# Attention, Fourier mix and FFN on one core: the second FFN matmul as seven block products in place of eight, for ten pairs of token chunks

## The chip, the core and the metric

The kernel runs on one core of a Trainium2 chip. The core has five engines, each with an instruction stream of its own: TensorE (PE; its weight loads are listed apart as PEld), VectorE (DVE), ScalarE (ACT), GpSimd (POOL) and SyncE (SP), which only issues transfers. They wait for one another by semaphores. Matmuls read SBUF and write PSUM, whose eight banks hold 512 fp32 values per partition. The metric is the time of one execution on the device in microseconds (us), less is better. The kernel before took 610.42, 608.97 and 610.12 us; the median is 610.12.

## The reference

Eight batches, 12 heads, 448 rows, 64 columns per head; D = 768 = 12 x 64; the FFN's inner width is 3072. All inputs and the output are fp32.

```python
scores = scale * np.matmul(q, k.transpose(0, 1, 3, 2))
attn = np.maximum(scores, 0.0) ** 2 / S
x = np.matmul(attn, v)                  # heads side by side: [8, 448, 768]
mixed = np.real(np.fft.fft(np.fft.fft(x, axis=1), axis=2))
u = x + mixed
un = (u - mean(u)) / np.sqrt(var(u) + 1e-06)
out = u + np.maximum(un @ w_ch1, 0.0) @ w_ch2      # 768 -> 3072 -> 768
```

The two FFN matmuls are done on 8 x 448 = 3584 rows, called tokens below.

## The kernel before

**How the order is made.** The program's order is written by a planner in Python that runs when the kernel is built. Each part of the work is a generator that asks for a step with `need(engine, duration, deps, bufs, ok)` (L104) and emits its instructions when the planner (`Streams.run`, L78) gives it its turn. The planner takes the step that could start first by its estimates; `ok` holds a step back while it is false. What comes out is one fixed order per engine, with semaphore waits between engines. On the chip every engine executes its own order strictly. SP's stores, loads and transposes are one such order, and GpSimd's loads and indirect stores are part of GpSimd's.

**Attention and mix, batch by batch.** Scores (L537, PSUM psS), relu (ACT, L558), square (DVE, L564), values (L522, PSUM psF). The result leaves PSUM as xT (DVE, L445 and L448); SP transposes it to rows, xn (L477); folds and differences (L456 to L468) halve the Fourier transform; the channel transform is L961, its copies pc L977, the row transform L805. A batch's half rows come in two chunks of 128 and 112. For each chunk and for top and bottom half, `mix_rows` makes qs (L811), tm and tp (L816), u = mix + xn (L825, L826, on POOL and DVE), statistics (L837, L838), std (L841), rstd (L844), nmr (L846) and un = u x rstd + nmr (L854, on POOL from batch 2). u and un go to DRAM: top rows from SP (L876), bottom rows in reverse order by indirect stores from POOL (L879). SP loads un back transposed as unT (L902), which is the moving operand of the first FFN matmul.

**The FFN in groups.** `ffn(b)` works on groups of 384 and 512 tokens in turn, eight in all; two groups cover two batches. A group's unT needs the un of its last batch. FFN1 (L1073): 24 inner blocks of 128, each six matmuls of 128 x N into one psF bank, then relu into hT (L1046 on ACT; L1044 on DVE for odd blocks of the first group). FFN2 (L1091): per chunk of 128 tokens and per half of 384 output columns, 24 matmuls accumulate in one psF bank, then DVE adds u, loaded into o by `reload` (SP, L1034), at L1054, and SP stores o (L1061). The last chunk of all is cut into 512 and 256 columns. PSUM: three two-bank tiles psS, two one-bank tiles psF.

**Attention between FFN work.** Attention steps of later batches (six scores, eight values matmuls) stand between FFN matmuls on TensorE. Their `ok` is a comparison of the FFN's progress with `lead`, the attention's progress less `LEAD = 1.9` batches. When the FFN of the group that needs batch b's un begins, TensorE's next FFN1 matmul waits for that unT; nothing of TensorE's order is moved for it.

**Buffers.** In SBUF: sq nine buffers, un four (two chunks by top and bottom), u two for each half, unT two, hT 24 tiles, o two of 768 columns.

Of the kernel before, what the change touches and what calls it, by code (L numbers as in the profile page):

```python
# [62 lines left out]
class Streams:  # L63
    def __init__(self):
        self.engine = dict.fromkeys(LATENCY, 0.0)
        self.streams = []
        self.dma_free = {"sw": 0.0, "hw": 0.0}
# [11 lines left out]
    def run(self):  # L79
        end = {}  # L80
        while self.streams:
# [7 lines left out]
            best = None  # L89
            for s in self.streams:  # L90
# [9 lines left out]
                if best is None or key < best[0]:  # L100
                    best = (key, s)
            if best is None:
                assert not self.streams, "stuck"
                break  # L104
            (_, start, _), s = best
# [32 lines left out]
def kernel(  # L138
# [26 lines left out]
    XH = 256  # L165

# [27 lines left out]
    warm = const.tile([128, 512], BF16, name="warm")  # L194
# [3 lines left out]
    dcol = work.tile([128, 2 * KH], FP32, name="dcol", tag="tm", bufs=1)  # L198
# [43 lines left out]
    def build_dft():  # L242
# [19 lines left out]
        f = work.tile([128, 4 * KH], FP32, name="dfty", tag="u", bufs=2)  # L262
        g = work.tile([128, 4 * KH], FP32, name="dfty", tag="u", bufs=2)
# [6 lines left out]
        for m in range(3):  # L270
            e = yield need("DVE", 1.5, [indices_ready])
            y = work.tile([128, 4 * KH], FP32, name="dfty", tag="u1" if m < 2 else "o", bufs=2)
            turns(y[:, 2 * KH:], y[:, 0:2 * KH], col2, row[:, 4 + m:5 + m], 2 * KH, m % 2)
            yield from sine(chan[m][:, 0, :], y[:, 0:2 * KH], 2 * KH, e, -1, halfpi)
            yield from sine(chan[m][:, 1, :], y[:, 2 * KH:], 2 * KH, e)
# [8 lines left out]
    BQ = [Bufs(QN), Bufs(QN), Bufs(3)]  # L284

    def load_group(i, which=(0, 1, 2)):
# [3 lines left out]
        for x, (nm, src) in enumerate((("q", q), ("k", k), ("v", v))):  # L290
# [5 lines left out]
            else:  # L296
                e = yield need("POOL", 0.85, bufs=[BQ[x]])
                t = work.tile([R, HG, 4 * Dh], BF16, name=f"{nm}n", tag=f"{nm}n",
                              bufs=3 if nm == "v" else QN)
# [19 lines left out]
    first_qk = [work.tile([128, NG, HG, 4 * Dh], BF16, name="qk0", tag="unT", bufs=2) for _ in range(2)]  # L319
# [43 lines left out]
    BSQ = Bufs(NSQ)  # L363
    BX = [Bufs(1) for _ in range(MC)]
# [5 lines left out]
    progress = [0.0]  # L370
# [6 lines left out]
    def turning():  # L377

        for b in range(B):
            for g in range(NG):  # L380
# [5 lines left out]
                for x in range(2):  # L386
# [3 lines left out]
                    BQ[x].free.append(e)  # L390
# [15 lines left out]
    def turn_on_pe(b, g):  # L406
# [23 lines left out]
        if b > 0:  # L430
            BQ[0].free.append(e1)
            BQ[1].free.append(e1)
        elif g == NG - 1:
            BUNT.free += [e1, e1]
# [4 lines left out]
    def fold(b, m, F, av, av_end):  # L439
        e1 = yield need("DVE", 2 * dve(HS) + 2 * dve2(NS), [av_end],  # L440
                        [BX[m]] + ([BA[m]] if m < 3 else []))
        x = xTc[m]

        at = av[:, 0:S].rearrange("q (j p) -> q p j", j=4)
        nc.vector.tensor_scalar(x[:, 0:HS].rearrange("q (p j) -> q p j", j=4), at[:, 0:R // 2],  # L445
                                1.0 / (64.0 * S), None, op0=ALU.mult)
        xb, ab = x[:, XH + 1:XH + NS].rearrange("q (p j) -> q p j", j=4), at[:, R - 1:R // 2 - 1:-1, ::-1]
        nc.vector.tensor_scalar(xb, ab, 1.0 / (64.0 * S), None, op0=ALU.mult)  # L448
        BF.give(av, e1 - 2 * dve2(NS))
        if b > 0:  # L450
            sch.add(turn_x(b, m, e1 - 2 * dve2(NS) + LATENCY["DVE"]), (1, 1))
        else:
            x_ready[b][m].t = e1 + LATENCY["DVE"]
        f = work.tile([128, 2, NS], BF16, name="fold", bufs=1,
                      tag=f"diff{m - 3}" if b == 0 and m >= 3 else f"fold{min(m, 3)}")
        nc.vector.tensor_tensor(f[:, 0, :], x[:, 0:NS], x[:, XH:XH + NS], op=ALU.add)  # L456
        nc.vector.tensor_tensor(f[:, 1, :], x[:, 0:NS], x[:, XH:XH + NS], op=ALU.subtract)
# [4 lines left out]
        elif m >= 3:  # L462
            i = m - 3
            e1 = yield need("DVE", 2 * dve2(2 * NS))
            t = work.tile([128, 2, NS], BF16, name="diff", tag=f"diff{i}", bufs=1)
            nc.vector.tensor_tensor(t, F[i], f, op=ALU.subtract)
            Bs[b].append(t)
            nc.vector.tensor_tensor(F[i], F[i], f, op=ALU.add)  # L468
# [13 lines left out]
    def attention(b):  # L482


        F, sqs, fresh = [], {}, []
        NB = 4 * MC
        p = pa = 0
        while pa < NB:
# [7 lines left out]
            n = max(0, min(n, NSQ - (p - pa - 4 * values)))  # L496
# [15 lines left out]
            e = yield need("PE", dur + SWITCH, deps, bufs, lambda: progress[0] >= lead and (b != 1 or tail[0] == 2 or tail[0] == 0 and p < 0))  # L512
            av_end, scs = None, []

            for part in ("scores", "values") if few else ("values", "scores"):
                if part == "values" and values:
                    av = BF.take()
                    vn, h0 = loads[b * NG + ma // 2][2], 2 * ma % HG
                    for c in range(4):
                        sq = sqs.pop(pa + c)[0]  # L520
# [26 lines left out]
            for i, _, _ in scs:  # L547
                sqs[i] = [None, Cell()]
# [5 lines left out]
    def squares(scs, sqs):  # L554
        for i, sc, t in scs:
            e = yield need("ACT", act(2 * S) - 0.03, [t + LATENCY["PE"]], [BSQ])
            r = sqs[i][0] = work.tile([R, 2, S], BF16, name="sq", tag="sq", bufs=NSQ)
# [9 lines left out]
    def attentions():  # L567
        for b in range(1, B):
            yield from attention(b)


    BU, BTS = [Bufs(2), Bufs(2)], Bufs(1)
    BPC, BUN = Bufs(1), [Bufs(1), Bufs(1)]
    group_ready = [Cell() for _ in range(B)]
# [4 lines left out]
    groups = []  # L579

    def first_tail(pcs):
# [70 lines left out]
        def copy(t, hf, en):  # L652
            ch, i = divmod(t, 2)
            n = SC[ch][1] - SC[ch][0]
            e = yield need(en, (act if en == "ACT" else dve)(D // 2), [done[t][hf]], [BU[i]] if hf == 0 else [])
            if hf == 0:
                uts[t] = work.tile([128, D], FP32, name="u", tag=f"u{i}" if i else "u", bufs=2)
# [127 lines left out]

    half_un, u_done = ([[Cell(), Cell()] for _ in range(2)] for _ in range(2))
# [10 lines left out]
    def mix_rows(b, ch, pcs):  # L797
# [14 lines left out]
        e = yield need("DVE", 2 * dve(KN), [e + LATENCY["ACT"]])  # L812
        ts = []
        for op, nm in ((ALU.subtract, "tm"), (ALU.add, "tp")):
            t = work.tile([128, 2 * KH], FP32, name=nm, tag=nm, bufs=1)
            nc.vector.tensor_tensor(t[:n, 0:KN], pq[:n, 0, 0:KN], qs[:n], op=op)  # L816
            ts.append(t)
# [3 lines left out]
        for i, eng, en, d in ((1, nc.gpsimd, "POOL", 1.8), (0, nc.vector, "DVE", 2 * dve(KN))):  # L821
            e1 = yield need(en, d, [e + LATENCY["DVE"]] + x_ready[b], [BU[i]])
            x = xns[b][:, 2 * i + ch, :]
            u = work.tile([128, D], FP32, name="u", tag=f"u{i}" if i else "u", bufs=2)
            eng.tensor_tensor(u[:n, 0:KN], ts[i][:n, 0:KN], x[:n, 0:KN], op=ALU.add)  # L825
            eng.tensor_tensor(u[:n, KN:D], ts[1 - i][:n, KN - 2:0:-1], x[:n, KN:D], op=ALU.add)  # L826
# [6 lines left out]
        for i, u in enumerate(us):  # L833
            e = yield need("DVE", 2 * dve(D // 2) + 0.2, [ut[i]])
            stats = work.tile([128, 2, 6], FP32, name="stats", tag="stats", bufs=2)
            for hf in range(2):
                nc.vector.bn_stats(stats[:n, hf, :], u[:n, hf * (D // 2):(hf + 1) * (D // 2)])  # L837
# [4 lines left out]
        e = yield need("DVE", 0.3, [e3 + LATENCY["ACT"]], [BUN[ch]])  # L842
# [5 lines left out]
        for i, u in enumerate(us):  # L848
# [3 lines left out]
            un = work.tile([128, D], BF16, name="un", tag=f"un{2 * ch + i}", bufs=1)  # L852
# [31 lines left out]
    def u_store(b, ch, us, ut, freed):  # L884
        yield from store_rows(ch, utop[b], ubot[b], us, 4, ut, u_stored[b])
        yield need("SP", 0.0, freed)
        for i in range(2):
            BU[i].free.append(max(u_stored[b][2 * ch + i].t, freed[i].t))

    def n_store(b, ch, t):  # L890
        yield from store_rows(ch, ntop[b], nbot[b], uns[b][2 * ch:2 * ch + 2], 2,
                              [t, t], n_stored[b])
        if b > 0:
            BUN[ch].free.append(n_stored[b][2 * ch + 1].t)

    def turn_un(b):

        def turn(g, c0, src, r0, w, deps, bufs=()):
            e = yield need("SP", 1.5, deps, bufs)
            if g is None:  # L900
                g = work.tile([128, MC, 512], BF16, name="unT", tag="unT", bufs=2)
# [3 lines left out]
        n = n_stored[b]  # L905
# [5 lines left out]
        elif b % 2 == 0:  # L911
            g, _ = yield from turn(None, 0, ntop[b], 0, HS, [n[0], n[2]], [BUNT])
            _, e = yield from turn(g, HS, nbot[b], 0, 384 - HS, [n[1], n[3]])
            groups.append((b * S, 384, g))
        else:
# [247 lines left out]
```

## Time and profile before

| | us |
|---|---|
| median of 3 runs (608.97 to 610.42) | 610.12 |
| span of the profiled execution | 607.4 |
| TensorE busy | 595.4 |
| VectorE busy | 339.4 |
| ScalarE busy | 293.3 |
| GpSimd busy | 155.2 |
| FFN1 matmuls L1073, busy | 227.2 |
| FFN2 matmuls L1091, busy | 225.0 |
| FFN groups begin at | 53.7, 126.7, 210.7, 272, 350.7, 413.5, 490.7, 541.7 |

The profiled execution's own span, 607.4 us, is from its first to its last instruction; the times of the runs include what lies around it. Busy times of groups of matmuls overlap a little, as matmuls are pipelined, and a few matmul records are missing. So one matmul's cost is read from the distance between the starts of two stretches, not from its duration.

### The profile page before, as it was taken

Reading aid. Unit: us, or ns where it says so; the run is one execution under the profiler, and the core shown is the slowest. Engines: PE = TensorE matmul, PEld = TensorE weight load, DVE = VectorE, ACT = ScalarE, POOL = GpSimd, SP = SyncE. Lnnn points to the kernel's source line nnn. Section 1 sums busy time; section 2 is a strip of 40 time slices with the busy share of each in tenths; the row PEclk is TensorE's granted clock in tenths of the full one; section 3 lists DMA queues with packets and bytes.
Section 4 is the critical chain, followed back from the end, with each engine's and each line's share of the span. In section 5 each row is a group of like instructions: output and inputs, shape, how many; then the busy total and the mean of one; then the engine's idle time right before and its main releaser. Section 6 shows DMA issues by size and latency. Waiting matters only on the chain.

```text
span 607.4 us, 10224 instructions
## 1 busy us (share of the span) xinstructions
PE 595.4 (98%) x4035; PEld 329.5 (54%) x4054; DVE 339.4 (56%) x766; ACT 293.3 (48%) x445; POOL 155.2 (26%) x200
## 2 busy tenths in 40 slices
PE   8999999989999999999999999999999999999997
PEld 7566556534555565555445565555445566654464
DVE  6977785876596568455834369645843447110011
ACT  5967661677544357436653167435761345014300
POOL 8433203311163137111710117210620006100000
PEclk9999999999999999999999999999999999999999
DMA  9999997888659967977593796985451215420022
GB/s 127 207 209 228 216 194 132 186 128 120 111 148 212 157 121 215 141 135 120 172 154 96 127 127 173 160 164 97 145 136 60 87 51 165 121 91 20 1 79 79
DMA packets 125216, 82.22 MB, mean 135 GB/s; under 512 B 76272, under 2 KB 113168, under 8 KB 125168
## 3 DMA queue, kind: packets, MB, share of 16 engines
q0 software_dynamic: 40320, 34.07, 34.4%
q1 hardware_dynamic: 84848, 47.50, 33.6%
q8 instruction: 32, 0.52, 0.4%
q14 instruction: 16, 0.13, 0.1%
HBM read 62.91 MB, written 26.69 MB: 148 GB/s over the span
## 4 chain that ended last, share of the span: by engine, by line
PE 83%; DVE 11%; ACT 4%; issue 1%; DVEq 0%; ACTq 0%
PE psF L1091 33%; PE psF L1073 32%; PE psF L522 6%; PE psS L537 6%; DVE sq L564 2%; PE psS L961 2%; ACT sq L558 2%; DVE stats L837 2%; PE psS L1113 1%; PE psS L805 1%; DVE u L826 1%; DVE u L825 1%; PE psS L605 1%; PE psF L421 1%; DVE tm L816 1%
## 5 line engine op out<-in xcount | busy, mean ns | idle before, releaser
L1073 PE MATMUL psF<-unT,w 128*128 128x384 bf16 (+1 forms) x1134 | 227.2, 352 | 1.4 <-issue 0.2
L558 ACT ACTIVATE sq<-psS 112x896 bf16<-112x896 f32 x192 | 164.8, 916 | 130.5 <-PE psS L537 130.4
L1091 PE MATMUL psF<-w,hT 128*128 128x384 bf16 (+2 forms) x1343 | 225.0, 326 | 0.8 <-DVE xT L448 0.7
L1091 PEld LDWEIGHTS <-hT 128*128 128x128 bf16 x1344 | 129.2, 98 | 93.4 <-issue 8.8
L1073 PEld LDWEIGHTS <-w 128*128 128x128 bf16 x1152 | 109.6, 98 | 109.3 <-issue 12.3
L1046 ACT ACTIVATE hT<-psF 128x512 bf16<-128x512 f32 (+1 forms) x180 | 98.6, 548 | 110.2 <-PE psF L1073 109.6
L564 DVE TENSOR_TENSOR sq<-sq 112x896 bf16<-112x896 bf16 x192 | 117.8, 635 | 44.6 <-ACT sq L558 43.3
L1054 DVE TENSOR_TENSOR o<-psF,o 128x384 f32<-128x384 f32 (+2 forms) x56 | 31.0, 553 | 106.2 <-PE psF L1091 105.9
L300 POOL DMA_DIRECT2D vn<-in_v_dram x24 | 17.3, 719 | 177.4 <-PE psF L522 156.9
L445 DVE TENSOR_SCALAR xT<-psF 128x224 bf16<-128x224 f32 x48 | 18.7, 389 | 71.7 <-PE psF L522 71.7
L537 PE MATMUL psS<-qkT 64*112 64x448 bf16 x384 | 52.3, 366 | 2.0 <-DVE unT L780 0.8
L522 PE MATMUL psF<-sq,vn 112*64 112x448 bf16 x384 | 45.9, 359 | 1.7 <-DVE sq L564 1.2
L825 POOL TENSOR_TENSOR u<-tp,xn 128x385 f32<-128x385 f32 (+1 forms) x14 | 15.5, 1108 | 117.0 <-DVE tp L816 94.7
L537 PEld LDWEIGHTS <-qkT 64*112 64x112 bf16 x384 | 20.8, 125 | 27.6 <-issue 21.6
L522 PEld LDWEIGHTS <-vn 112*64 112x64 bf16 x384 | 17.9, 109 | 24.2 <-issue 16.0
L854 POOL TENSOR_SCALAR un<-u,rstd,nmr 128x768 bf16<-128x768 f32 (+1 forms) x24 | 26.9, 1124 | 6.4 <-DVE nmr L846 6.0
L837 DVE BATCH_NORM_STATS2 stats<-u 128x6 f32<-128x384 f32 (+1 forms) x56 | 28.2, 539 | 0.0
L879 POOL DMA_INDIRECT ubot<-u,back x16 | 17.1, 1072 | 23.7 <-DVE hT L1044 19.3
L300 POOL DMA_DIRECT2D qn<-in_q_dram x21 | 15.3, 726 | 19.7 <-DVE qkr L389 10.8
L1113 PE MATMUL psS<-warm 128*128 128x126 bf16 (+1 forms) x204 | 17.9, 242 | 1.3 <-DVE warm L215 1.3
L448 DVE TENSOR_SCALAR xT<-psF 128x224 bf16<-128x224 f32 x48 | 18.4, 384 | 0.0
L456 DVE TENSOR_TENSOR fold<-xT 128x225 bf16<-128x225 bf16 x48 | 15.9, 331 | 2.1
(117 smaller groups left out, 369.1 us busy)
## 6 DMA issues: line engine op xcount, KB each, us to landing
out_dram<-o SPq DMA_DIRECT2D x27, 384.0 KB, 2.7
vn<-in_v_dram POOLq DMA_DIRECT2D x24, 224.0 KB, 5.0
qn<-in_q_dram POOLq DMA_DIRECT2D x21, 224.0 KB, 6.3
kn<-in_k_dram POOLq DMA_DIRECT2D x21, 224.0 KB, 7.2
w<-in_moe_w_ch_dram POOLq DMA_DIRECT2D x12, 384.0 KB, 14.1
w<-in_moe_w_ch_dram POOLq DMA_DIRECT2D x4, 1152.0 KB, 22.7
utop<-u SPq DMA_DIRECT2D x8, 384.0 KB, 2.6
o<-utop SPq DMA_DIRECT2D x8, 384.0 KB, 4.5
```

Of the source, the lines that this page charges most:

```text
L300: nc.gpsimd.dma_start(out=t, in_=src[b, hs].rearrange("h (p j) d -> p h (j d)", j=4))
L522: nc.tensor.matmul(av[h * Dh:(h + 1) * Dh, 0:S], lhsT=vn[:, c, h0 + h, :], rhs=sq[:, h, :], start=(c == 0), stop=(c == 3))
L537: nc.tensor.matmul(sc[:R, h, 0:S].rearrange("k (c q) -> k c q", c=4), lhsT=kT[ps, m % 2, c, :], rhs=qT[ps, m % 2], start=True, stop=True)
L558: nc.scalar.activation(r, sc[:R, :, 0:S], AF.Relu)
L564: nc.vector.tensor_tensor(r, r, r, op=ALU.mult)
L837: nc.vector.bn_stats(stats[:n, hf, :], u[:n, hf * (D // 2):(hf + 1) * (D // 2)])
L854: nc.gpsimd.tensor_scalar(un[:n], u[:n], rstd[:n, i:i + 1], nmr[:n, i:i + 1], op0=ALU.mult, op1=ALU.add)
L1046: nc.scalar.activation(h[:, 0:N], ph[:, 0:N], AF.Relu)
L1054: nc.vector.tensor_tensor(o[:, hs], pc[:, 0:w], o[:, hs], op=ALU.add)
L1073: nc.tensor.matmul(ph[:, 0:N], lhsT=w1_sb[m][hf][:, jj * 128:(jj + 1) * 128], rhs=unT[:, m, 0:N], start=(m == 0), stop=(m == MC - 1))
L1091: nc.tensor.matmul(pc[:, 0:w], lhsT=hT[j][:, c * 128:(c + 1) * 128], rhs=w2_sb[j // 6][:, j % 6, hs], start=(j == 0), stop=(j == JC - 1))
L1113: nc.tensor.matmul(first_pps[0][:, t, c0:512], lhsT=warm[:, 0:128], rhs=warm[:, c0:512], start=not begun, stop=False)
```

## The change

Split the 16 first inner blocks into eight pairs (even, odd), the 768 output columns into two halves, and take two chunks of 128 tokens, L and R. Then these 16 blocks of FFN2 are a product of a 2 x 2 by a 2 x 2 matrix of blocks, in which each block product is eight matmuls of 128 x 384. The usual way needs eight block products. The new one needs seven (Winograd's form), with sums of the operands:

- of the weights, once (`weight_sums`, 32 adds of 128 x 384 on POOL): T3 = B22 - B12, T2 = T3 + B11, T4 = B21 - T2, and T1 = B12 - B11 in place over the weights themselves;
- of the hidden values, per pair, on DVE: s1 = R_even + R_odd, s2 = s1 - L_even, and R_even replaced by L_even - R_even (`early`); L_odd replaced by L_odd - s2 after product b1 has read it (`late`). Each is made in two pieces, of 768 and of 256 columns;
- of the products, in PSUM and in the output tiles: a bank is added to one output tile, then goes on accumulating the next product, is added to the next tile, and so on. Eight adds per pair in place of four.

The other eight inner blocks (`rest`) are done as before. TensorE's order in a pair is a1 (8 matmuls), b1 (16), a2 (8), b2 (8), a3 (8), b3 (16), a4 (16), b4 (8): 88 matmuls in place of 96. It is done for ten pairs in the groups that are not `PLAIN`; FFN2 goes from 1344 to 1264 matmuls of 384 columns.

With it come:

- nine groups of 384, 512, 256, 512, 512, 512, 256, 512 and 128 tokens. In FFN1 two inner blocks share a bank where N is 256, four where it is 128;
- room for the sums: the weight sums lie in unT0 (so one unT tile is left from the third group on), in two u and u1 buffers, in two sq buffers and in the first q and k buffers. From batch 3 on both chunks of a batch use one pair of un buffers and one pair of u buffers; sq has six buffers in place of nine. tm is no longer a tile of its own, qs is overwritten. s1 and s2 lie in the other un buffers;
- hT as one tile [128, 24, 512]; the output in pieces of 384 columns in six slots, each loaded, added to and stored by itself (`outputs`). SP has 262 instructions in place of 193;
- `load_left`: four loads on POOL bring back the weights that T1 has overwritten, for the last, plain group;
- in the planner: LEAD 2.3, `APART` (the gated attention steps at least 1.3 us of FFN work apart), `fill` (a gated attention step is taken early when TensorE's next step would otherwise start over 0.5 us later), and from batch 3 the steps of fold and mix_rows are planned one instruction at a time (`next_step`).

TensorE's order is the same as before up to the second group's FFN1.

```diff
+    GT = [0, 384, 896, 1152, 1664, 2176, 2688, 2944, 3456, B * S]
+    KP = 8
...
+            if best[1][2][0] == "PE" and spare is not None and best[0][1] - spare[0][1] > 0.5:
+                best = spare
...
+        room = NSQ if b < 3 else NSQ - 3
...
+    def side(b, ch):
+        return ch if b < 3 else 1
...
-        e = yield need("DVE", 0.3, [e3 + LATENCY["ACT"]], [BUN[ch]])
+        e = yield need("DVE", 0.3, [e3 + LATENCY["ACT"]], [BUN[ch if b < 3 else 0]])
...
-            un = work.tile([128, D], BF16, name="un", tag=f"un{2 * ch + i}", bufs=1)
+            un = work.tile([128, D], BF16, name="un", tag=f"un{2 * (ch if b < 3 else 0) + i}", bufs=1)
...
+    PLAIN = (0, 1, NGR - 1)
+    CH = [(0, 6), (6, KP)]
...
+    def weight_sums():
...
+        def each(n, outs, xs, ys, op, deps):
+            T[n] = outs
+            for i in range(KP):
+                e = yield need("POOL", 1.3, deps)
+                nc.gpsimd.tensor_tensor(outs[i], xs[i], ys[i], op=op)
+            sums[n].t = e + LATENCY["POOL"]
...
+        yield from each(3, t3, b22, b12, ALU.subtract, [])
...
+        yield from each(2, t2, t3, b11, ALU.add, [sums[3]])
...
+        yield from each(4, t4, b21, t2, ALU.subtract, [sums[2]])
+        yield from each(1, b12, b12, b11, ALU.subtract, [w2_free, sums[3]])
...
+    def outputs(slot):
+        for g, c, hf, at in uses():
...
+            e = yield need("SP", 0.1, stored + [ffn_begun[g]])
...
+                nc.sync.dma_start(out=o[t - t0:t - t0 + w], in_=src[r:r + w, cs])
...
+            e = yield need("SP", 0.1, [added[g, c, hf]])
+            nc.sync.dma_start(out=rows[t0:t0 + 128, cs], in_=o)
...
+        for j in range(0, JC, JN):
...
+            for i in range(JN):
+                for m in range(MC):
+                    nc.tensor.matmul(ph[:, i * N:(i + 1) * N], lhsT=w1_sb[m][hf][:, (jj + i) * 128:(jj + i + 1) * 128],
+                                     rhs=unT[:, m, 0:N], start=(m == 0), stop=(m == MC - 1))
...
+        def early(self):
...
+                nc.vector.tensor_tensor(s1, h[:, ev, R_], h[:, od, R_], op=ALU.add)
+                nc.vector.tensor_tensor(s2, s1, h[:, ev, L], op=ALU.subtract)
+                nc.vector.tensor_tensor(h[:, ev, R_], h[:, ev, L], h[:, ev, R_], op=ALU.subtract)
...
+        def late(self):
...
+                nc.vector.tensor_tensor(h[:, self.od[k], L], h[:, self.od[k], L], made[1][k], op=ALU.subtract)
...
+        def chain_a(self):
...
+            self.product(pc, self.block(0, self.L), self.weights(0, 0), True)
+            t = yield from self.add(pc, e, c, 0, False, False)
...
+            self.product(pc, self.formed(1), T[2], False)
+            t = yield from self.add(pc, e, c + 1, 0, False, False)
...
+            self.product(pc, self.formed(0), T[1], False)
+            t = yield from self.add(pc, e, c + 1, 1, False, False)
+            e = yield need("PE", d + dr, [t] + self.r4 + self.ht[2 * KP:])
+            self.product(pc, self.block(1, self.L), self.weights(1, 1), False)
+            self.rest(pc, self.L, 1, False)
+            yield from self.add(pc, e, c, 1)
...
+        def chain_b(self):
...
+            self.product(pc, self.block(1, self.L), self.weights(1, 0), True)
+            self.rest(pc, self.L, 0, False)
+            yield from self.add(pc, e, c, 0)
...
+            self.product(pc, self.block(0, self.R), T[3], True)
+            t = yield from self.add(pc, e, c + 1, 1, False, False)
...
+            self.product(pc, self.block(1, self.R), T[4], False)
+            self.rest(pc, self.R, 0, False)
+            yield from self.add(pc, e, c + 1, 0)
...
+            self.rest(pc, self.R, 1, True)
+            yield from self.add(pc, e, c + 1, 1)
...
-    LEAD = 1.9
+    LEAD = 2.3
...
+        sch.fill = lambda: progress[0] > 2.0
```

More of the change, by code (lines that the diff above doesn't have):

```diff
@@ L439, in fold @@
     def fold(b, m, F, av, av_end):
[L440 to L447, printed above, removed]
@@ L811, in mix_rows @@
         nc.scalar.activation(qs[:n], pq[:n, 1, 0:KN], AF.Copy)
[L812 to L817, printed above, removed]
+        e = yield need("DVE", (2 if b < WHOLE else 1) * dve(KN), [e + LATENCY["ACT"]])
+        tp = work.tile([128, 2 * KH], FP32, name="tp", tag="tp", bufs=1)
+        nc.vector.tensor_tensor(tp[:n, 0:KN], pq[:n, 0, 0:KN], qs[:n], op=ALU.add)
+        e = yield from next_step(b, "DVE", dve(KN), e)
+        nc.vector.tensor_tensor(qs[:n], pq[:n, 0, 0:KN], qs[:n], op=ALU.subtract)
+        ts = [qs, tp]
         BS.give(pq, e)
@@ L1068, in ffn, with add @@
-        for j in range(JC):
+            for x in ht[j:j + JN]:
+                x.t = e + LATENCY["ACT"]
+        def add(pc, e, c, hf, last=True, give=True):
+            e = yield need("DVE", dve(DH), [e + LATENCY["PE"], ot[b, c, hf]])
+            o = os[b, c, hf]
+            nc.vector.tensor_tensor(o, pc[:, 0:DH], o, op=ALU.add)
+            if give:
+                BF.give(pc, e)
+            if last:
+                added[b, c, hf].t = e + LATENCY["DVE"]
+            return e + LATENCY["DVE"]
```

394 lines of the change are left out of this document (285 added, 109 removed).

## The prediction

> **What bounds the kernel now.** I read the page's busy shares and slices first.
>
> ```profile
> PE 595.4 (98%) x4035; PEld 329.5 (54%) x4054; DVE 339.4 (56%) x766; ACT 293.3 (48%) x445; POOL 155.2 (26%) x200
> ...
> PE   8999999989999999999999999999999999999997
> ...
> DVE  6977785876596568455834369645843447110011
> ...
> PEclk9999999999999999999999999999999999999999
> ```
>
> TensorE is busy for 595.4 of 607.4 us at a full granted clock. Of the 12 us left, about 8 lie before 158 us, so there is no idle time left to win behind it: time falls if TensorE gets less work, and rises with every new wait of TensorE. The profiled execution spans 607.4 us and the median of the runs is 610.12, so 2.7 us lie around the span; I sum against 607.4 and add 2.7.
>
> Next the timeline, for durations. Columns: start, duration, engine, line, operation.
>
> ```profile
> 48.33 0.71 PE L706 MATMUL psS<-warm 128*128 128x256 bf16 x5
> 48.88 0.34 PE L708 MATMUL psS<-rev,un 128*128 128x63 bf16 x6
> 49.05 1.06 PE L713 MATMUL psS<-warm 128*128 128x128 bf16 x16
> 49.94 0.49 PE L706 MATMUL psS<-warm 128*128 128x256 bf16 x3
> ...
> 502.62 15.86 PE L1073 MATMUL psF<-unT,w 128*128 128x384 bf16 x96
> ...
> 518.31 23.56 PE L1091 MATMUL psF<-w,hT 128*128 128x384 bf16 x144
> ...
> 541.71 31.24 PE L1073 MATMUL psF<-unT,w 128*128 128x512 bf16 x141
> 572.79 31.36 PE L1091 MATMUL psF<-w,hT 128*128 128x384 bf16 x191
> ```
>
> From start to start: FFN2, 144 matmuls of 384 columns, 518.31 to 541.71, 0.1625 us each. FFN1 at 384: 15.69/96 = 0.163; at 512: 31.08/144 = 0.216. The rows of 48 to 50 us give 0.11 (256 columns) and 0.056 (128 columns, each with its own weight load).
>
> Last the way of a batch's second chunk of rows into the next group, for batches 3 and 7.
>
> ```profile
> 236.86 0.16 DVE L846 SCALAR_TENSOR_TENSOR nmr<-mv,rstd 112x2 f32<-112x2 f32 x1
> 237.13 2.51 POOL L854 TENSOR_SCALAR un<-u,rstd,nmr 112x768 bf16<-112x768 f32 x2 [0.38 <-DVE nmr L846]
> 239.91 1.03 POOL L879 DMA_INDIRECT nbot<-un,back  x1 [0.28 <-POOL un L854]
> 244.30 3.26 SPq L902 DMA_TRANSPOSE unT<-nbot  x1
> 247.65 4.05 SPq L477 DMA_TRANSPOSE xn<-xT  x2
> ...
> 514.22 0.16 DVE L846 SCALAR_TENSOR_TENSOR nmr<-mv,rstd 112x2 f32<-112x2 f32 x1
> 515.57 1.93 POOL L854 TENSOR_SCALAR un<-u,rstd,nmr 112x768 bf16<-112x768 f32 x2
> 518.15 0.96 POOL L879 DMA_INDIRECT nbot<-un,back  x1 [0.65 <-POOL un L854]
> 521.28 1.33 SPq L902 DMA_TRANSPOSE unT<-nbot  x1
> ```
>
> ```profile
> DMA to landing us min/median/max: 2.5/4.3/8.9
> ```
>
> That last line is of the unT transposes (L902), the rows below of busy time by stretch (PE, PEld, DVE, ACT, POOL).
>
> ```profile
> 126.70:157.90 31.20, 31.04 (x166) 13.31 (x169) 18.11 (x44) 22.11 (x33) 5.73 (x9) 1.00 0.89 126
> 157.90:210.70 52.80, 52.04 (x343) 28.22 (x343) 36.43 (x82) 24.64 (x34) 17.65 (x18) 1.00 0.82 158
> ...
> 350.70:413.50 62.80, 62.55 (x419) 35.21 (x418) 42.67 (x93) 33.42 (x55) 19.19 (x21) 1.00 0.88 153
> ```
> In batch 7 the second chunk's transpose lands near 525 (521.28 + 3.4) and group 7 begins at 541.71: 16 us of slack. The change shortens the work that covers this way.
>
> **The change, part by part.**
>
> *FFN2's products.* A pair takes 56 + 32 = 88 matmuls in place of 96; ten pairs drop 80. 80 x 0.1625 = **-13.0 us**, all on TensorE.
>
> *FFN1's columns.* Before: 576 x 0.163 + 576 x 0.216 = 218.3. After: 144 x 0.163 + 720 x 0.216 + 288 x 0.11 + 144 x 0.056 = 218.7: **+0.4**. The 128-column group is the uncertain one: were its matmuls paced like the mix's (24 of 193 columns in 2.0 us, 0.083), it would add 3.9 more. I take 0.056, as that burst also loads weights each time, and keep 0 to +4. [...]
>
> *VectorE.* A pair costs 8 adds of 0.553 (L1054's row) in place of 4, and 8 bf16 sums: four of 768 elements, four of 256, by the squares' row (896 in 0.635) 0.54 and 0.2. That is 5.2 us more per pair, 52 in all. It is hidden while VectorE keeps up: from 350.7 to 413.5 it is busy 42.7 of 62.8; with two pairs 53.1 of about 60, 88%. It doesn't bound, but queues get longer. Inside a pair each product of chain a waits for the add behind the one before (handoff 0.25 + add 0.55 + 0.1 = 0.9) while the other chain's product covers 8 x 0.1625 = 1.3. Cover suffices unless the add stands behind a square (0.635) or a mix operation (u 0.55, bn 0.54): then it misses by 0.2 to 0.8. Some five pairs have such work beside them; I take **+1.4** (0 to 4).
>
> *GpSimd.* 32 weight sums (bf16, 128x384) run between about 126 and 220 us. GpSimd's add of 385 fp32 columns takes 0.9 to 1.3, so 29 to 42 us in a stretch where GpSimd is busy 23 of 84: they fit. But two-input adds on both engines stretch each other: VectorE's u at 503.68 takes 0.55, at 504.14, beside GpSimd's u (503.85, 1.15), 1.27. Lower bound 0 (VectorE is busy 54.5 of the 84); upper, 3. I take **+1.0**. [...]
>
> *Group 2 is 256 tokens long, and group 3 needs batch 3's second chunk.* Only one pair of FFN2 lies between. By the instruction order of the changed kernel, VectorE does nmr of that chunk behind the add that follows a4, the seventh of eight product blocks. TensorE has after a4: values 0.95, scores 0.78, b4 1.3, values 0.95, scores 0.78 = 4.8, and then the first matmul of group 3. From a4's end to unT: handoff, add, rstd, nmr 0.25 + 0.55 + 0.16 + 0.16; to un 0.3; un 1.93 to 2.51; nbot's issue 0.3 later, to the transpose's start 3.1 (518.15 to 521.28) to 4.4; landing 2.5 to 6.5 (what the batch-2 transpose took). Sum 9.3 to 15.1, with the median landing of 4.3 about 11.8: TensorE waits 7. A second way gives the same: on SP's queue this transpose is behind an xn transpose that waits for xT copied from the last values, so -0.78 + 0.25 + 0.78 (two xT) + 1.22 + 1.33 + 4.3 = 7.1. Batch 7's landed in 3.4, so I take 3.3, a us less: **+6.0** (4.0 to 10). Nothing fills it: TensorE's order is fixed.
>
> *Group 6 is 256 tokens long, group 7 needs batch 7's second chunk.* On SP the nbot7 transpose stands behind the output store of b4, the pair's last product, which waits for its add; group 7's first matmul comes right after b4. So the wait is 0.25 + 0.55 + store issue 0.35 + 0.2 + landing 2.5 to 4.3 = 3.9 to 5.7. The data is no earlier: both chunks now use one un and one u pair of buffers, so the second waits until the first's stores have landed (ubot 4.4 us, nbot 3.5 after issue). **+4.8.** In the same pair b2 waits for an add behind u and bn: **+0.5**.
>
> *Other homes.* Six sq buffers instead of nine from batch 3, one unT tile: groups 4, 5 and 8 have 4 us and more between data and use by the same counting, since 512 tokens of work lie between; 0. The output's 384-column pieces make SP issue 262 instead of 193; a store is 0.35 and SP is waited for nowhere else that I counted: 0. Four loads on GpSimd's queue (0.72 each) bring back original weights for the last group while GpSimd is idle (its slices read 0 at the end): 0.
>
> *Tail.* The last add is 384 columns (0.55 for 0.42) and the last store 192 KB, between 1.7 (128) and 2.0 (256): **+0.4**.
>
> Sum: -13.0 + 0.4 + 1.4 + 1.0 + 6.0 + 4.8 + 0.5 + 0.4 = +1.5: span 608.9. With 2.7 around it **611.6**.
>
> **The rivals.**
>
> *The waits are hidden (faster).* It needs batch 3's and 7's chunks to be done before a4 resp. b4, which VectorE's and SP's order speaks against; yet attention work is taken early in the new order, and a start of each chain some 6 us earlier than I read it would do. Then -13.0 + 0.4 + 1.4 + 1.0 + 0.4 = -9.8: 600.3. With one of the two waits gone: 605.6 to 606.8.
>
> *VectorE becomes the bound inside pairs (slower).* At 88% with a fixed order, each handoff takes a square and a mix operation more (1.2 us); from the point where 8 matmuls no longer cover it, five of the ten pairs lose about 1 us at three of their handoffs: +15 less the 1.4 counted. With the sum's other terms: about 617 where half of it comes, 625 in full.
>
> *The 128-column FFN1 is paced by loads.* 611.6 + 3.9 = 615.5.
>
> *The saving doesn't arrive, as the products are paced by weight loads:* a load is 98 ns beside 162 of a matmul, so no; 2%.
>
> **How the numbers follow.** Forecast (both waits, little else) 0.42; one or both waits gone 0.30; VectorE's handoffs or ports 0.20; load-paced FFN1 0.06, other 0.02. The bounds of the terms all short give 605, all long about 625; 8 in 10 lies in 602 to 619, the forecast's own range is 608 to 615. 0.3% (1.8 us) is about what a measurement of this kernel can tell from no change. Faster: 0.30 and 0.05 of the forecast: 0.35. Within: 0.15. Slower: 0.50.
>
> **What would show it.** FFN2 rows of 384 columns fall from 1344 to 1264 and busy TensorE by about 13 us. A gap of 5 to 7 us on TensorE ahead of the fourth group's first matmul, some 38 us after the third group's start, with a unT transpose landing at its end, and one of 4 to 6 us ahead of the eighth group; between them gaps under 1 us released by the adds. VectorE near 390 busy. If the first gap is absent, the prediction is too high by its size; if VectorE's adds release more than 4 us in all, too low.

## The result and the profile after

The changed kernel takes **629.79 us** (median of 4 runs, 626.63 to 636.0), the kernel before 610.27 (608.97 to 611.09): a ratio of 1.0338, 95% interval 1.0281 to 1.0396 (the quotient of the two medians, 1.0320, lies inside it). By the medians it is 19.5 us slower. The forecast was 611.6 with a range of 602 to 619. The profiled execution spans 626.6 us, 19.2 more than the one of before; the four executions took 626.63, 628.35, 631.22 and 636.0 us, and the longer one took, the lower was its mean granted clock (0.984, 0.980, 0.976, 0.970).

Busy shares and slices of the changed kernel:

```profile
PE 591.0 (94%) x4118; PEld 331.3 (53%) x4118; DVE 401.7 (64%) x886; ACT 293.2 (47%) x427; POOL 188.2 (30%) x236
...
PE   8999999899999989579999999999999999699997
...
DVE  6977787846599867726598565975687759101520
...
PEclk9999999999999889979999999999999999899999
```

Two things are new. TensorE is idle for 35.6 us (626.6 - 591.0) where it was idle for 12.0, and the row of the granted clock, all 9s before, has 8s in it. TensorE's busy time fell by 4.4 us only, not by the 13.0 of the 80 matmuls.

What TensorE waited for, in the changed kernel (us in total, times, longest):

```profile
PE psF L1222 <- DMA unT<-nbot: 15.8, 3, 10.4
PE psS L1035 <- DVE fold L511: 2.9, 1, 2.9
PE psF L573 <- DVE o L1209: 2.3, 1, 2.3
PE psF L1222 <- ACT unT L840: 1.7, 1, 1.7
```

The four large waits on the timeline (the first line above holds two of them; start, duration, instruction; in brackets the idle time before it and what ended it):

```profile
204.94 1.19 PE L573 MATMUL psF<-sq,vn 112*64 112x448 bf16 x8 [2.34 <-DVE o L1209]
226.45 0.34 PE L1035 MATMUL psS<-chan,fold 128*128 128x193 bf16 x1 [2.88 <-DVE fold L511]
270.87 5.48 PE L1222 MATMUL psF<-unT,w 128*128 128x512 bf16 x18 [10.35 <-DMA unT<-nbot]
544.24 34.20 PE L1222 MATMUL psF<-unT,w 128*128 128x512 bf16 x144 [4.97 <-DMA unT<-nbot]
```

They add to 20.5 us. The last two are the fourth and the eighth group's waits for unT. And look at the durations behind them: 144 matmuls of 512 columns take 34.2 us here and took 31.1 before; 18 take some 5.4 where 18 x 0.216 = 3.9. The granted clock in two-us stretches (PE's busy time, clock, DMA share, GB/s) says why:

```profile
540.00:542.00 2.00, 0.00 (x0) 1.00 0.87 200
542.00:544.00 2.00, 0.00 (x0) 0.86 0.92 187
544.00:546.00 2.00, 1.76 (x5) 0.50 0.69 196
546.00:548.00 2.00, 2.00 (x6) 0.50 0.61 184
548.00:550.00 2.00, 2.00 (x6) 0.50 0.62 176
550.00:552.00 2.00, 2.00 (x10) 0.94 0.00 0
```

The clock drops to half during this wait, and it stays there for some 6 us of work, which costs half of that. Behind the shorter wait at 205 us the drop came only after its end, at 205.5; the last section shows when the clock changes.

The sum of the 19.2 us: matmuls -13.0 (FFN2) and +0.4 (FFN1); idle time +23.6, of it 20.5 in the four waits; and the rest of TensorE's busy time, -4.4 + 12.6 = **+8.2**, is put down to matmuls at half clock. The stretches at half clock right behind the four waits account for 7.6 of it (1.7, 1.5, 1.4 and 3.0).

Why did an output add and a fold come late at 205 and 226 us? VectorE and GpSimd beside each other:

```profile
197.08 5.90 DVE L618 TENSOR_TENSOR sq<-sq 112x896 bf16<-112x896 bf16 x1
197.25 5.24 POOL L1104 TENSOR_TENSOR wsum<-w,wsum 128x384 bf16<-128x384 bf16 x6
...
221.45 3.90 DVE L497 TENSOR_TENSOR fold<-xT 128x225 bf16<-128x225 bf16 x1
221.70 3.50 POOL L1104 TENSOR_TENSOR w<-w 128x384 bf16<-128x384 bf16 x4
```

One square, which usually takes 0.63 us, took 5.90 beside six weight sums of GpSimd; one fold of 0.28 took 3.90 beside four. Each ends within 0.5 us of the end of GpSimd's series. The output add and the fold that TensorE needs stand behind them.

Last, the fourth group's wait. TensorE is done at 260.5. SP's queue and the indirect store before it:

```profile
258.19 1.02 POOL L943 DMA_INDIRECT nbot<-un,back  x1 [0.28 <-POOL un L918]
...
260.09 1.27 SPq L424 DMA_TRANSPOSE qkT<-qkr  x1
...
261.46 1.27 SPq L520 DMA_TRANSPOSE xn<-xT  x1
...
262.82 3.59 SPq L972 DMA_TRANSPOSE unT<-ntop  x1
...
266.50 1.33 SPq L972 DMA_TRANSPOSE unT<-nbot  x1
```

TensorE goes on at 270.87, when the last transpose has landed. That transpose was issued 8.3 us after nbot's store, behind two other transposes and one into unT that held the queue for 3.59. The store itself had landed after 3.2 us, at 261.4, so the data lay ready for 5.1 us.

### The profile page after: what moved, and what is told of

Read it like the earlier page. It is cut to its first block, busy times and chain, and to the rows that moved or that the text cites. A ratio compares the mean times of both kernels' runs of the same rounds, so it can differ in the third digit from the quotient of the medians.

```text
span 626.6 us, 10716 instructions
## 1 busy us (share of the span) xinstructions
PE 591.0 (94%) x4118; PEld 331.3 (53%) x4118; DVE 401.7 (64%) x886; ACT 293.2 (47%) x427; POOL 188.2 (30%) x236
## 4 chain that ended last, share of the span: by engine, by line
PE 71%; issue 10%; DVE 9%; DMA 3%; ACT 3%; POOL 2%; SPq 1%; POOLq 0%; DVEq 0%; ACTq 0%
PE psF L1222 33%; PE psF L1312 16%; PE psF L1255 7%; PE psF L573 5%; PE psS L588 5%; DVE sq L618 3%; DMA unT<-nbot 2%; PE psS L1035 2%; ACT sq L612 2%; PE psS L866 1%; SPq L972 1%; DVE o L1209 1%; DMA out_dram<-o 1%; DVE fold L497 1%; PE psS L665 1%
## 5 line engine op out<-in xcount | busy, mean ns | idle before, releaser
L1222 PE MATMUL psF<-unT,w 128*128 128x512 bf16 (+3 forms) x1296 | 231.9, 336 | 17.6 <-DMA unT<-nbot 15.8
L1222 PEld LDWEIGHTS <-w 128*128 128x128 bf16 x1296 | 118.7, 99 | 121.8 <-issue 17.9
L1200 ACT ACTIVATE hT<-psF 128x512 bf16<-128x512 f32 (+1 forms) x162 | 95.5, 590 | 152.0 <-PE psF L1222 150.8
L618 DVE TENSOR_TENSOR sq<-sq 112x896 bf16<-112x896 bf16 x192 | 131.4, 699 | 35.5 <-ACT sq L612 34.5
L1312 PE MATMUL psF<-w,hT 128*128 128x384 bf16 x560 | 96.0, 326 | 0.0
L1312 PEld LDWEIGHTS <-hT 128*128 128x128 bf16 x720 | 69.6, 98 | 49.1 <-issue 3.7
L1209 DVE TENSOR_TENSOR o<-psF,o 128x384 f32<-128x384 f32 x96 | 53.0, 552 | 65.7 <-PE psF L1312 50.3
L1255 PE MATMUL psF<-w,hT 128*128 128x384 bf16 x376 | 66.2, 329 | 0.5 <-DVE o L1209 0.5
L1255 PEld LDWEIGHTS <-hT 128*128 128x128 bf16 x384 | 36.7, 98 | 28.1 <-issue 5.3
L474 DVE TENSOR_SCALAR xT<-psF 128x224 bf16<-128x224 f32 x48 | 18.7, 389 | 43.1 <-PE psF L573 42.9
L1293 DVE TENSOR_TENSOR s<-hT 128x768 bf16<-128x768 bf16 (+1 forms) x20 | 8.8, 438 | 33.3 <-ACT hT L1200 32.6
L1312 PE MATMUL psF<-wsum,hT 128*128 128x384 bf16 x160 | 29.3, 326 | 0.1
```

The costliest lines, as they stand in the source:

```text
L618: nc.vector.tensor_tensor(r, r, r, op=ALU.mult)
L1200: nc.scalar.activation(hs, ps, AF.Relu)
L1209: nc.vector.tensor_tensor(o, pc[:, 0:DH], o, op=ALU.add)
L1222: nc.tensor.matmul(ph[:, i * N:(i + 1) * N], lhsT=w1_sb[m][hf][:, (jj + i) * 128:(jj + i + 1) * 128], rhs=unT[:, m, 0:N], start=(m == 0), ...
L1255: nc.tensor.matmul(pc[:, 0:DH], lhsT=h[:, j, c * 128:(c + 1) * 128], rhs=left[j // 2] if swap else w2(j, hf), start=(j == 0), stop=(j == J ...
L1312: nc.tensor.matmul(pc[:, 0:n], lhsT=lhs[i], rhs=rhs[i], start=(start and i == 0), stop=(i == k - 1), skip_group_check=True)
```

## The experiments

Three theories stand against one another. Theory A: the matmuls are saved as forecast, and lost again in four waits and in the half clock behind them; two waits come from small groups whose unT is late, two from GpSimd's sums that hold up VectorE. Theory B: VectorE has too much work for the products. Theory C: the loss is in group sizes and homes of buffers. Ratios are to the kernel before, run on the same chip.

### 1. Matmuls that fill two waits

```diff
             ph = BF.take()
+            for i in range({3: 40, 7: 18}.get(b, 0) if j == 0 else 0):
+                nc.tensor.matmul(ph[:, 0:512], lhsT=w1_sb[0][0][:, 0:128], rhs=w1_sb[0][0][:, 0:512],
+                                 start=True, stop=True)
```

> The changed kernel, with 40 matmuls of 512 columns on constant data put ahead of the fourth group's first FFN1 matmul and 18 ahead of the eighth group's, where TensorE waits 10.35 and 4.97 us for unT; their results are overwritten, all else is unchanged. They take 8.6 and 3.9 us at full clock and fit in the waits. Theory A (the loss is four waits of TensorE, 20.5 us, and matmuls that run at half clock behind each wait, some 8 us): behind these two waits the clock cost 1.5 and 3.0 us (18 matmuls of 512 columns in 5.40 instead of 3.9 us, 144 in 34.0 instead of 31.1), so the time falls by 4 to 4.5 us, to 625 to 626. Theory B (VectorE has too much work, and everything runs late behind it; the clock has nothing to do with the waits): no change, 630.

Measured: 623.94 us, ratio 1.0231 (1.0204 to 1.0257): **5.9 us less** for 58 matmuls more; 625 to 626 was expected. The order of everything else is that of the changed kernel. On its timeline:

```profile
226.41 0.26 PE L1035 MATMUL psS<-chan,fold 128*128 128x193 bf16 x1 [2.88 <-DVE fold L511]
...
269.46 4.06 PE L1225 MATMUL psF<-unT,w 128*128 128x512 bf16 x18 [1.67 <-DMA unT<-nbot]
...
541.73 31.25 PE L1225 MATMUL psF<-unT,w 128*128 128x512 bf16 x144 [1.01 <-DMA unT<-nbot]
```

18 and 144 matmuls are at full speed again: 1.4 and 3.0 us. Some 1.4 of the rest were not won by the filling: behind the same 2.88 us wait at 226 the clock stayed full in this execution (the first matmul takes 0.26, 0.34 in the changed kernel). The last section shows why. The half clock behind waits is shown, and that it goes with the idle time (from 264 to 272 us the granted clock is 1.00 here and 0.50 in the changed kernel); theory B's "no change" falls.

### 2. The weight sums on VectorE

```diff
-                e = yield need("POOL", 1.3, deps)
-                nc.gpsimd.tensor_tensor(outs[i], xs[i], ys[i], op=op)
-            sums[n].t = e + LATENCY["POOL"]
+                e = yield need("DVE", dve2(DH), deps)
+                nc.vector.tensor_tensor(outs[i], xs[i], ys[i], op=op)
+            sums[n].t = e + LATENCY["DVE"]
```

> The changed kernel with the 32 weight sums on VectorE instead of GpSimd. Theory A: the two waits ahead of the third group (2.34 for an output add at 205 us, 2.88 for a fold at 226 us) come from single VectorE operations that took 5.9 and 3.9 us beside a series of GpSimd's sums; without the series both go, and with them the clock's cost behind them (1.7 and 1.4 us): 8 us less, 621 to 623. Theory B: VectorE gets 12 us more (32 by about 0.37), in the part where it is 75% busy, and the time rises to 632 or more.

Measured: 618.8 us, ratio 1.0147 (1.0116 to 1.0178): **11.0 us less**. VectorE gets 32 operations more and is busy for *less* time, 394.2 us for 401.7. Its squares and one quarter of the sums there:

```profile
L618 DVE TENSOR_TENSOR sq<-sq 112x896 bf16<-112x896 bf16 x192 | 119.9, 637 | 36.8 <-ACT sq L612 35.7
L1104 DVE TENSOR_TENSOR wsum<-wsum,w 128x384 bf16<-128x384 bf16 x8 | 2.9, 397 | 0.0
```

In the changed kernel the squares' mean is 699 ns. A sum takes 0.35 to 0.40 us here and 0.87 to 1.1 on GpSimd. Both waits of 2.3 and 2.9 us are gone. This is theory A's mechanism, with more weight than it gave it (621 to 623 was expected); B expected a loss. The planner made a new order for this run, so the 11.0 us hold the price of the new order too; run 12 makes the opposite move.

### 3 and 4. Groups and homes without the products

```diff
-    PLAIN = (0, 1, NGR - 1)
+    PLAIN = tuple(range(NGR))
...
-        sch.add(weight_sums(), (6, 6))
-        sch.add(load_left(), (6, 6))
```

> The changed kernel with no products and no sums: all nine groups do FFN2 in the plain way; group sizes, homes of buffers, output pieces and planner stay. Theory A: 13 us of matmuls come back, the two waits of the sums go, the wait of the fourth group stays, as 29 us of TensorE's work lie between batch 3's row transform and that group (27 in the changed kernel, 52 with the old group sizes), the wait of the eighth group goes (46 in place of 23): 615 to 621. Theory B: VectorE is back at its old load, about 611. Theory C (the groups and homes cost it all): 13 us more than the changed kernel, above 635.

Measured: 622.93 us, ratio 1.0195 (1.0162 to 1.0228). Above the range given; the fourth group waits 6.69 us and the clock is at half behind it (0.50 from 257 to 263 us), and an output add costs 2.11:

```profile
259.07 4.80 PE L1222 MATMUL psF<-unT,w 128*128 128x512 bf16 x12 [6.69 <-DMA unT<-nbot]
...
338.06 1.47 PE L573 MATMUL psF<-sq,vn 112*64 112x448 bf16 x8 [2.11 <-DVE o L1209]
```

The eighth group does not wait: without the products the planner put batch 7's row transform 46 us of TensorE's work ahead of it.

```diff
-    GT = [0, 384, 896, 1152, 1664, 2176, 2688, 2944, 3456, B * S]
+    GT = [0, 384, 896, 1280, 1792, 2176, 2688, 3072, B * S]
```

> As the run before, with the old eight groups of 384 and 512 tokens in turn: what is left of the change are the homes of buffers, the output in 384-column pieces, the single hT tile and the planner's changes. Theory A: these cost little, 610 to 613. Theory C, if it is the homes: above 620.

Measured: 615.62 us, ratio 1.0087 (1.0065 to 1.0108). Expected was 610 to 613: homes, output pieces and planner together cost 5 us, not nothing. In the profiled execution, one wait of 2.49 us for xT and the half clock behind it (12 matmuls of 512 columns in 4.45 us, where 12 x 0.216 = 2.6) are most of it. So of the 3.4% slower, some 0.9 are there with old groups, 1.1 more come with the new group sizes (third run against fourth), and the products with their sums bring 1.4 more, though they save 13 us of matmuls. Part of theory C holds by this: 2.0 of the 3.4% are there without a single product.

### 5. The planner is told of the wait

The planner gives a group's first FFN1 step no dependence on unT; it saw no wait there.

```diff
-            e = yield need("PE", 6 * JN * mm(N), [w1_ready[hf]], [BF])
+            e = yield need("PE", 6 * JN * mm(N), [w1_ready[hf], group_ready[b]], [BF])
```

> The weight sums on VectorE (as in the second run), and the planner is told that TensorE's first FFN1 step of a group waits for unT, so that it takes attention steps early there. Theory A: TensorE's work between batch 3's row transform and the fourth group goes from 24 to 29 us, its wait from 9.6 to 4 to 5 us; the eighth group's from 4.9 to about 3; with less of the clock's cost behind them 611 to 613, from 618.8. Rival (the wait is set by VectorE and SP, which slow down as TensorE's cover grows): 617 to 619.

Measured: 612.81 us, ratio 1.0054 (1.0034 to 1.0075); 6.0 less than the second run. The fourth group's wait is 4.95 us (from 9.58), as expected; the eighth's 4.29, where about 3 was expected. More of TensorE's own work ahead of the group shortens the wait, but not one for one. From the end of the row transform to the fourth group it went from 22.7 to 29.0 us, and the wait fell by 4.6; at the eighth it went from 22.3 to 24.8, and the wait fell by 0.6. The rival holds in part: nbot's store for the fourth group was issued 24.4 us after the row transform, 20.5 in the second run.

### 6. The transposes into unT first in SP's queue

Their planned dependence was set 6 us early (the real waits stay), so that they are placed ahead of stores and other transposes.

> The weight sums on VectorE, and SP's order changed: the transposes into unT for the fourth and the eighth group stand ahead of the stores of output and of the transposes of qkT and xn that stood before them. Theory A, with its detail that SP's queue ends both waits (in the second run the last transpose is issued 9.4 us after the store of un that it reads, at 256.7, and at the eighth group 5.1 us): 1.3 us less at the fourth group, as its landing of ntop is then next to be waited for, and 1.3 at the eighth: 615.5 to 616.5. Rival (the data is late anyway): 618.8.

Measured: 616.91 us, ratio 1.0113 (1.0085 to 1.0142), 1.9 less than the second run and 0.4 above the range expected. The waits are 7.25 (9.58) and 3.75 (4.90): SP's queue is part of both, and the edit did not empty it. Ahead of the fourth group nbot's store landed at 252.77, and its transpose was issued at 256.24, behind ntop's (2.10) and a store of output (0.57). So of the 7.25 us some 3.5 are still SP's queue, and 3.1 lie between the last transpose's issue and TensorE's next matmul.

### 7 and 8. Fold and mix planned in whole steps again

```diff
-    WHOLE = 3
+    WHOLE = B
```

The seventh run has this with the sums on VectorE and both edits before it.

> Sums on VectorE, the planner told of the wait for unT, the transposes first, and fold and mix planned in whole steps for all batches, as in the kernel before. TensorE's work between a batch's row transform and the group that needs it: 31 us at the fourth group, 44 at the eighth. Theory A: a wait of 1 to 4 us at the fourth group, none at the eighth, 604 to 608: faster than the kernel before. Theory B (VectorE too full for the products): 612 or more.

Measured: 609.42 us, ratio 0.9995 (0.9981 to 1.001): level with the kernel before. The fourth group waits 2.95 us, the eighth not at all, as expected; but the time was to be 604 to 608. TensorE was idle for 22.2 us of 607.3: besides 2.95, there are new waits behind ScalarE:

```profile
441.39 1.46 PE L1236 MATMUL psF<-unT,w 128*128 128x512 bf16 x6 [0.74 <-ACT hT L1214]
444.07 0.95 PE L587 MATMUL psF<-sq,vn 112*64 112x448 bf16 x8 [1.23 <-ACT hT L1214]
```

> The old groups without products, with fold and mix planned in whole steps for all batches as before. In the run with old groups 2.5 us were lost where xT stood on VectorE behind a copy that waited for a transpose of qkT, and 1.9 behind it to the clock. If the planning in single steps put it there: 610 to 611.5. If the homes of buffers did: 615.

Measured: 610.69 us, ratio 1.0017 (1.0001 to 1.0033). With whole steps the old groups lose 0.2% instead of 0.9%. So the new homes, the output pieces and the planner's other changes (`LEAD`, `APART`, `fill`), which no run takes apart, cost about 1 us together (0 to 2 by the interval), and the order that the planner made with single steps cost the rest of the fourth run's loss. (All edits to the planner change the whole order; this is the cost of that order, not of one step.)

### 9. The seventh run without products

> The seventh run's kernel without products and sums (plain FFN2 in all nine groups), planned again. Theory A: the 13 us of matmuls come back, and the small waits at the pairs' adds go; between 35 us and more of TensorE's work ahead of each group leave no wait of over 2 us: 611 to 617, so the products are then worth 2 to 8 us. Theory B (VectorE's extra work eats the saving wherever it is put): 606 to 609.5, no slower than with products.

Measured: 612.53 us, ratio 1.0035 (1.0015 to 1.0054), 3.1 more than with products. TensorE is busy for 598.0 us against 585.1, and idle for 13.3 against 22.2. The mean granted clock is 0.994 in both. So the products do save 12.9 us of TensorE, and in the seventh run 8.9 us of that go into idle time.

### 10 and 11. Two of those waits taken out

Ten matmuls on constant data ahead of the fourth group, then also ScalarE's std step planned later:

```diff
-        e3 = yield need("ACT", 0.25, [e + LATENCY["DVE"]])
+        e3 = yield need("ACT", 0.25, [e + LATENCY["DVE"] + (1.2 if b > 2 else 0.0)])
```

> The seventh run's kernel with 10 matmuls of 512 columns on constant data ahead of the fourth group's first FFN1 matmul (2.15 us, in a wait of 2.95); results overwritten. Theory A (the clock halves in a wait of this length): behind this wait the profile of the seventh run has the clock at half for a while, so 1 to 1.7 us less, about 608. Rival: no change, 609.4.

Measured: 608.14 us, ratio 0.9966 (0.9946 to 0.9985), 1.3 less than the seventh run, as expected; the intervals of the two touch, so this alone settles little.

> As the run before, with the ScalarE step for std planned 1.2 us later from batch 3 on, so that relu steps stand ahead of it where std waits for VectorE's statistics (1.10 us at 443 us in the seventh run, with relu and so TensorE behind it). Theory A: 3.4 us of TensorE's idle time between 350 and 450 shrinks by 1 to 2: 606 to 607.5, faster than the kernel before. Rival (the waits move elsewhere): 608 and more.

Measured: **604.96 us**, ratio 0.9908 (0.9876 to 0.994): the fastest of all, 0.9% faster than the kernel before, and 1 us below the range expected. TensorE's waits for ScalarE's hT fell from 3.3 us in all to 1.2. But the two profiled executions differ by 1.1 us only (604.9 and 603.8); the rest of the 3.2 between the medians no trace shows. Its longest waits:

```profile
PE psF L1239 <- ACT unT L854: 1.7, 1, 1.7
PE psF L1329 <- DVE o L1223: 1.5, 2, 0.9
PE psS L1409 <- DVE warm L244: 1.3, 1, 1.3
```

The first and the third were there in the seventh run too; the waits of the products' matmuls for an add, the second, come to 1.5 us. VectorE is busy for 397.7 us, hardly less than in the changed kernel. Theory B falls with this: the same work on VectorE, and TensorE waits little for it.

### 12. The sums back on GpSimd in the best kernel

> The kernel of the eleventh run with the 32 weight sums back on GpSimd, planned again. Theory A (a series of GpSimd's sums holds up two-input operations of VectorE, and TensorE behind them): 6 to 11 us more, 611 to 616, with waits of TensorE of 2 us and more between 150 and 230 us and VectorE's squares and folds of 3 to 6 us beside the sums. Rival (in the second run it was the new order that helped, not the engine): within 2 us of the eleventh run.

Measured: 619.7 us, ratio 1.0148 (1.0112 to 1.0184): **14.7 us more** than the run before. VectorE, GpSimd, and what TensorE waited for:

```profile
201.73 6.03 DVE L632 TENSOR_TENSOR sq<-sq 112x896 bf16<-112x896 bf16 x4
...
221.26 5.63 DVE L511 TENSOR_TENSOR fold<-xT 128x225 bf16<-128x225 bf16 x1
```

```profile
197.71 6.90 POOL L1118 TENSOR_TENSOR wsum<-w,wsum 128x384 bf16<-128x384 bf16 x6
...
221.51 5.24 POOL L1118 TENSOR_TENSOR w<-w 128x384 bf16<-128x384 bf16 x6
```

```profile
PE psS L1049 <- DVE fold L525: 4.6, 1, 4.6
PE psF L1272 <- DVE o L1223: 3.1, 1, 3.1
PE psF L587 <- DVE o L1223: 2.2, 2, 1.8
```

One fold takes 5.63 us beside six sums, as in the changed kernel, and TensorE waits 4.6 for the folds. The four squares of the first line are another case: there squares and sums mostly take turns (squares of 1.33 where 0.63 is usual, sums of 1.28 where 0.9 is), until the last square is held for 2.74 beside two sums. Of the 14.5 us between the profiled executions of runs 11 and 12, 11.0 are idle time of TensorE. VectorE's total rises to 408.8 us with 32 operations fewer. The place of 32 small sums, with the order that the planner makes of it, decides between 0.9% faster and 1.5% slower than the kernel before. It was more than expected (611 to 616), and the rival (within 2 us) falls.

## Why the prediction was wrong

The forecast called slower the likeliest outcome (0.50) and had most of its mechanisms right, but it missed the size by 18 us. Two steps failed: the price of GpSimd's sums, and the clock, which had no term. Step by step:

- **FFN2's products, -13.0: right.** Runs 7 and 9 differ by 12.9 us of TensorE's busy time.
- **FFN1's columns, +0.4: right**, including the uncertain term: the 144 matmuls of 128 columns run from 606.87 to 614.91, 0.056 each. The rival "paced by loads" (+3.9) falls.
- **GpSimd, "+1.0" (0 to 3): the step that failed.** The price was taken from one pair of operations (0.55 stretched to 1.27), with sums that "fit" into GpSimd's idle time. In a series it can be another matter: one VectorE operation took 5.90 us beside six sums, another 3.90 beside four, and each ended within 0.5 us of the series. In the changed kernel that made two waits of 5.2 us together, and some 3.2 of half clock behind them. The place of the sums was worth 11.0 us in the second run and 14.7 in the twelfth, with the planner's new orders in both. The chances named "ports" (in the 0.20 with VectorE's handoffs), but no sum priced them above 3. No run shows a port; what the runs show is these times of the two engines beside each other.
- **The clock: a term that was missing.** Every wait was priced at its length. In the profiled execution 8.2 us were lost at half clock, 4.4 of them behind the fourth and eighth group's waits as run 1 shows. The rows of before that the forecast read, with a clock of 1.0, could not show it.
- **The fourth group, +6.0 (4 to 10): mechanism right, size off.** It was 10.35, just outside its own bounds. The second way of counting, by SP's queue, was the right one. It gave 7.1, which the forecast then lowered to 6.0 for a short landing; the landing was 4.3 as first counted. It lacked a qkT transpose ahead (about 0.7) and 2.3 us for the transpose from ntop, which held the queue for 3.59 and not for 1.33. Such a long hold stood among the quoted lines of before (3.26 at 244.30).
- **The eighth group, +4.8: right** (4.97), and by the step that was given: the nbot7 transpose was issued at 541.06, behind the store of b4.
- **VectorE inside pairs, +1.4 and +0.5: right in size.** TensorE's waits for output adds, the one behind the sums left out, come to 1.4 us, the largest 0.87; the rival "VectorE becomes the bound" falls with runs 2 and 11.
- **Other homes, 0: about right** with whole planning steps (run 8, +0.2%), but the planner's single steps, listed in the change and given no price, cost a further 0.7% with the old groups (run 4).

The terms close the account of the profiled execution, 626.6 against 608.9: 8.2 for the clock, 4.2 for the two waits behind GpSimd's sums (5.2 in place of 1.0), 4.4 for the fourth group, 0.2 for the eighth, and 0.7 for the rest.

Both failed steps have one form: a cost was read where the events were rare (one GpSimd operation, no long wait) and used where they were not.

## What to carry to other kernels

Price a wait of the matmul engine at its length plus the slow matmuls behind it: here 20.5 us of waits were followed at once by a loss of 7.6. Small elementwise work put on an idle engine is not free: here 32 sums on GpSimd, with the orders planned for them, cost 11.0 and 14.7 us more than on VectorE, and a VectorE operation beside them took 5.90 us where 0.63 is usual. Look at the neighbour's longest single operation, not at either engine's load. And where a planner writes the order, check that it sees every wait: telling it of the wait for unT (run 5) gave 6 us.

## What the runs showed of the hardware

- Within each run's trace all changes of the granted clock lie on one grid of 3.41 us, and for two waits it was decisive where they fell on it. In the changed kernel the stretches at half clock behind the four waits last 3.41, 3.41, 10.24 and 6.83 us, all multiples of 3.41; they begin at 205.51, 225.99, 263.54 and 543.43, which lie 6, 11 and 82 times 3.41 apart. Of the 2.88 us wait at 226 us, 2.42 lie in one stretch of it in the changed kernel; in run 1 the grid cuts the wait into 1.77 and 1.11. The stretches there, changed kernel first (length, PE's busy time, clock, DMA share, GB/s):

```profile
222.58:225.99 3.41, 0.99 (x10) 1.00 1.00 178
225.99:229.41 3.42, 2.96 (x19) 0.50 0.71 173
```

```profile
221.89:225.30 3.41, 1.63 (x16) 1.00 0.93 129
225.30:228.71 3.41, 2.31 (x27) 1.00 0.77 215
```

- Over all fourteen traces, a stretch of 3.41 us at full clock in which TensorE was busy for less than 40% was followed by half clock in 24 of 24 cases, and one above 62% never was; between them it was in 6 of 22, and what decides there no run shows. In the changed kernel TensorE was busy for 31, 29, 11 and 0% of the stretches ahead of the four drops; after one of 57%, from 181.62, the clock stayed full. A wait of 1.73 us at 124 us left the clock full in the changed kernel, where the grid divides it (stretches of 68 and 69%), and was followed by 0.50 in run 7, behind a stretch of 58%.
- A two-input VectorE operation can last as long as a whole series of GpSimd's additions, not as one: 5.90 us beside six, 3.90 beside four, 5.63 beside six in run 12, where 0.63 (the square) and 0.28 (the folds) are usual. In these three VectorE's operation began first by the profile (197.08 against 197.25, 221.45 against 221.70, 221.26 against 221.51). It is not always so: beside the four sums from 214.15 in the changed kernel, squares took 0.86 to 1.33 and the sums up to 1.47, in turns. What decides between the two was not tried.
- Of the 95 transposes that SP issued in the changed kernel, 78 held its queue for 1.2 to 1.4 us, but 10 for 1.8 to 4.6. These are of all kinds: from ntop ahead of the fourth group 3.59, from nbot at 414.6 4.61, qkT at 113.2 2.69. Why was not tried.
